# Grouping the expert work of a fused attention and mixture-of-experts kernel behind two of every three attention steps

## The chip, the cores and the metric

The kernel runs on one core of a Trainium2 chip. The metric is the device time of one execution in microseconds, as a median over runs. A profile is one further execution with the hardware profiler on; its own span is a little shorter than its device time, because the span runs from the first to the last instruction.

Five engines matter here. TensorE (PE in the views; PEld is its weight load) does matrix multiplies. VectorE (DVE) and ScalarE (ACT) do elementwise work, GpSimd (POOL) does one cast per step and issues the weight loads, and SyncE (SP) issues most other DMAs.

## The reference

Multi-query attention, 8 batches, 16 query heads that share one key and value head, 384 tokens, head size 64. The result is read as 3072 token rows of 1024 numbers and goes through a two-level mixture of experts: four groups, four experts in each, one expert per token.

```python
scores = scale * np.matmul(q, k.transpose(0, 1, 3, 2))
attn = softmax(scores)
x = np.matmul(attn, v)          # (B, H, S, D) -> rows (B*S, H*D)
...
g_idx = np.argmax(x @ w_group, axis=1)
e_idx = np.argmax(xg @ w_expert[g], axis=1)
h = np.maximum(xg[mask_e] @ w1[g, e], 0.0)
out[tok_idx] = (g_w * e_w)[:, None] * (h @ w2[g, e])
```

The kernel is built on the case that nearly all tokens of a batch choose the same expert: per batch it takes the most frequent expert of the first 128 tokens and runs all 384 tokens through it, gated. A single leftover pair of batch and expert is handled at the end in a compact form, and anything more in a rare block that these inputs do not enter.

## The kernel before

**Steps.** The attention is cut in 24 steps, `p = 0..23`, three for each batch `b` (`st = 0, 1, 2`: the opening, the middle and the last step of the batch). A step covers 128 query rows of all 16 heads. The whole order of work is written out by hand, and each engine executes its instructions in that order.

In step `p`, TensorE computes six score tiles (`scores`, L251, groups of four 64x64 matmuls in fp32) and, interleaved with them, the six value products of the step before (`values`, L290, accumulated in one PSUM tile `o`). The order is S0 S1 S2, V0 S3, V1 S4, V2, a small `join` (L273), S5, V3, V4, V5, where S belongs to step `p` and V to step `p-1`. ScalarE takes an exponential over each score tile (L253), then squares the raw queries for a later range check (`stats_q`, L209), and in the last step of a batch the keys also (`stats_k`, L213).

VectorE adds up the six exponentials (`pre_add`, L259 and L261), inverts the sums of the step before (L278, L280), multiplies the values product by them (`weigh`, L300, which frees `o`), folds its own sum (L265), and **turns**, that is transposes, the queries of the next step (`prep_q`, L243) and the keys of the next batch (`prep_k`, L233). In the text before the change these turns stand right behind S0 S1 S2 of each step.

**Phases.** Behind each step from the fifth on stands a phase of expert work. It is made of units, taken one by one from a queue by `fill(1)` (L451). A batch has 14 units: eight `h` units (L407, one 128-column block of the first layer, eviction on ScalarE in L408) and six `y` units (L415, eviction on ScalarE in L416, scaled by the gates `gsel`). Phases have four or five units; `FIVES` (L497) lists the steps with five. Three units are taken inside step 4.

**Gates.** In the phase of a middle step stand two further things. `gates(b)` (L466) multiplies the attention output by the gating weights (L312), and VectorE works out the choice of the expert and the gates (L318 to L382), with one exponential `ex` on ScalarE in between (L371). `counts(b, None)` (L333) counts the choices with one matmul (L338), copies the count on ScalarE (L342) and picks the expert on VectorE (L352); GpSimd then issues the loads of its weights. In the last step's phase `counts(None, b-1)` (L340, L342) and `gate_c` (L386 to L395) give `gsel` for the batch before.

**Buffers.** All PSUM tiles apart from `o` come from one pool of three (`side`, L76). A new tile waits for the last reader of the tile whose place it takes: an exponential, an eviction, a count copy, or VectorE's inversion.

**Loads.** In a middle step SyncE issues the keys of the next batch (L107), eight pieces of its queries (L92) and its values (L113), behind the stores of finished rows (L436).

Of the kernel before, what the change touches and what calls it, by code (L numbers as in the profile page):

```python
# [21 lines left out]
def kernel(  # L22
# [12 lines left out]
    B, H, S, D = q.shape  # L35
# [6 lines left out]
    ST = S // P  # L42
# [33 lines left out]
    def side(shape, dtype, name):  # L76
        return ps_s.tile(shape, dtype, tag="s", name=name)
# [20 lines left out]
    def some_q(n=1):  # L98
        for _ in range(n):
            if q_todo:  # L100
                q_todo.pop(0)()
# [129 lines left out]
    def prep_k(b):  # L231
        kT[b] = pool.tile([P, S], FP32, tag="kT", name="kT")
        nc.vector.transpose(out=kT[b][:], in_=k_raw[b][:].rearrange("p k d -> p (k d)"))  # L233

    def q_of(p):
        b, st = divmod(p, ST)
        if b == 0:
            return q_raw[0][:, st].rearrange("p h a d -> p h (a d)")
        return q_raw[b][:, :, st * (P // 32):(st + 1) * (P // 32)].rearrange("p h k d -> p h (k d)")

    def prep_q(p):
        qT[p] = pool.tile([P, 2 * CW], FP32, tag="qT", bufs=2, name="qT")
        nc.vector.transpose(out=qT[p][:].rearrange("p (h n) -> p h n", h=HP), in_=q_of(p))  # L243
# [71 lines left out]
    def gate_logits(b, ps, lo, hi):  # L315
        if lo == 0:
            logits[b] = pool.tile([P, ST, 32], FP32, tag="L", bufs=2, name="L")
        nc.vector.transpose(out=logits[b][:, lo:hi, :].rearrange("p s e -> p (s e)"), in_=ps[:, lo * 32:hi * 32])  # L318
# [14 lines left out]
    def counts(now, full):  # L333
        n = GE * (1 + ST)
        ps = side([P, n], FP32, "cps")
        lo, hi = (0 if now is not None else GE), (n if full is not None else GE)
        if now is not None:
            nc.tensor.matmul(out=ps[:, 0:GE], lhsT=ones_bf[:], rhs=first[now][:].rearrange("p g e -> p (g e)"), start=True, stop=True)  # L338
        if full is not None:
            nc.tensor.matmul(out=ps[:, GE:n], lhsT=ones_bf[:], rhs=ohe_t[full][:].rearrange("p s g e -> p (s g e)"), start=True, stop=True)  # L340
        t = pool.tile([P, n], FP32, tag="cnt1", bufs=2, name="cnt1")
        nc.scalar.copy(out=t[:, lo:hi], in_=ps[:, lo:hi])  # L342
        if now is not None:
            seen[now] = t[:, 0:GE]
            choose_b(now, t[:, 0:GE])
        if full is not None:
            gate_c(full, t[:, GE:n])

    def choose_b(b, cnt):
        top = pool.tile([P, 8], FP32, tag="top", bufs=1, name="top")  # L350
        idx = pool.tile([P, 8], U32, tag="idx", bufs=2, name="idx")
        nc.vector.max_with_indices(out_max=top[:], out_indices=idx[:], in_=cnt)  # L352
        reg = nc.values_load(idx[0:1, 0:1], engines=(ET.Pool,), min_val=0, max_val=GE - 1, skip_runtime_bounds_check_because="an index into 16 counts")
        w1 = wpool.tile([P, KO, F], BF16, tag="w1", name="w1")
        load_w1(w1, reg)
        w2 = wpool.tile([P, FO, Dm], BF16, tag="w2", name="w2")
        nc.gpsimd.dma_start(out=w2[:], in_=w2f[bass.ds(reg, 1)].rearrange("a p k f -> (a p) k f"))
        wts[b] = (w1, w2)
        choice[b] = idx
# [79 lines left out]
    NP = B * ST  # L439
# [26 lines left out]
    def gates(b):  # L466
        if b == 0:
            choose_a(0, gate_a(0, 0, 1))
            return
        ps = gate_a(b, 0, ST)  # L470
        choose_a(b, ps)
        gate_logits(b - 1, ps, 1, ST)
        gate_math(b - 1)
# [20 lines left out]
        nc.vector.tensor_copy(out=oki[:], in_=okf[:])  # L494
        bound["okf"] = okf

    FIVES = (8, 10, 12, 14, 16, 18, 19, 21, 22)  # L497
    leftover = {}

    def early_pair():  # L500
        last = B - 1
        mask = pool.tile([P, GE], FP32, tag="mask", bufs=1, name="mask1")
        idf = pool.tile([P, 1], FP32, tag="idf", bufs=1, name="idf1")
        nc.vector.tensor_copy(out=idf[:], in_=choice[last][:, 0:1])
        nc.vector.tensor_scalar(out=mask[:], in0=iota16[:], scalar1=idf[:, 0:1], scalar2=None, op0=OP.is_equal)
        nc.vector.scalar_tensor_tensor(out=extra[:, last * GE:NPAIR], in0=seen[last], scalar=0.0, in1=mask[:], op0=OP.is_gt, op1=OP.subtract)
        known = pool.tile([P, 1], FP32, tag="known", bufs=1, name="known")
        nc.vector.reduce_sum(out=known[:], in_=extra[:], axis=AX)
        top = pool.tile([P, 8], FP32, tag="top", bufs=1, name="top2")
        idx = pool.tile([P, 8], U32, tag="idx2", bufs=1, name="idx2")  # L510
        nc.vector.max_with_indices(out_max=top[:], out_indices=idx[:], in_=extra[:])
        pf = pool.tile([P, 1], FP32, tag="pf", bufs=1, name="pf")
        nc.vector.tensor_copy(out=pf[:], in_=idx[:, 0:1])
        base = pool.tile([P, 1], U32, tag="base", bufs=1, name="base")
        nc.vector.tensor_scalar(out=base[:], in0=idx[:, 0:1], scalar1=NPAIR - GE, scalar2=None, op0=OP.bitwise_and)
        basef = pool.tile([P, 1], FP32, tag="basef", bufs=1, name="basef")
        nc.vector.tensor_scalar(out=basef[:], in0=base[:], scalar1=float(S // GE), scalar2=None, op0=OP.mult)
        gi = pool.tile([P, ST, 2], FP32, tag="gi", bufs=1, name="gi")
        nc.vector.tensor_scalar(out=gi[:, :, 1], in0=tokid[:], scalar1=basef[:, 0:1], scalar2=None, op0=OP.add)
        reg = nc.values_load(idx[0:1, 0:1], engines=(ET.Pool, ET.DVE, ET.SP), min_val=0, max_val=NPAIR - 1, skip_runtime_bounds_check_because="an index into 128 flags")  # L520
        leftover.update(known=known, pf=pf, gi=gi, reg=reg)
# [16 lines left out]
    for p in range(NP):  # L538
        b, st = divmod(p, ST)
        jobs = [lambda: gates(0), lambda: None, lambda: counts(0, None)] if p == 2 else []  # L540
        if p == 0 or p == ST or (st == 1 and 1 < b < B - 1):
            load_q(b + 1)
        for j in range(3):
            scores(p, j)
            if p == 0 and j == 0:
                turn_q(1, lambda h: q_raw[0][:, 1, h], [nc.vector.tensor_copy])
        if p == 0:
            stats_k(0)
            prep_k(1)
        elif 2 < p < NP - 1:  # L550
            prep_q(p + 1)
            if st == 2:
                prep_k(b + 1)
        if jobs:
            jobs.pop(0)()
        for j in (1, 2):
            pre_add(p, j)
        for j in range(KB):
            if p > 0:
                values(p - 1, j)  # L560
            if j == 2 and p > 0:
                join(p - 1)
            if j + 3 < KB:
                scores(p, j + 3)
            if 0 < j < 4:
                pre_add(p, j + 2)
            if j == 2 and p > 0:
                invert(p - 1)
            if j == 3:
                stats_q(p)  # L570
                if p == 1:
                    turn_q(2, lambda h: q_raw[0][:, 2, h], [nc.scalar.copy])
                elif p == 2:
                    turn_q(3, lambda h: q_nat[0][:, h], [nc.scalar.copy])
            if jobs:
                jobs.pop(0)()
            if p == ST + 1 and j == 0:
                fill(3)
            if st == 1 and 0 < b < B - 1 and j == 0:
                load_k(b + 1)  # L580
            if 0 < j < 5:
                some_q(1 if p <= ST + 1 else 2)
            if st == 1 and b + 1 < B and j == KB - 1:
                load_v(b + 1)
        assert not jobs
        if p > 0:
            weigh(p - 1)
        fold_keys(p)
        if st == 2 and b + 1 < B:
            stats_k(b + 1)  # L590
        if p > ST:
            n = 5 if p in FIVES else 4
            steps = {}
            if p == NP - 1:
                bound_a()
            if st == 2:
                steps = {0 if b == 1 else 1: lambda: counts(None, b - 1)}
                if p == NP - 1:
                    steps = {0: lambda: (counts(None, b - 1), early_pair()), n - 1: bound_b}
            if st == 1:  # L600
                steps = {n - 2: lambda: gates(b), n - 1: lambda: counts(b, None)}
            for i in range(n):
                fill(1)
                if i in steps:
                    steps[i]()
# [250 lines left out]
```

## Time and profile before

| what | us |
|---|---|
| device time, three runs | 465.73, 466.64, 466.73 |
| device time of the profiled execution | 466.36 |
| its span | 464.9 |
| TensorE matmuls busy | 452.9 |
| VectorE busy | 305.4 |
| ScalarE busy | 243.0 |
| GpSimd busy | 60.4 |

The mean granted clock of TensorE was 0.995 of full speed. In the list of groups the first column is a line of the kernel, then come engine, operation, tiles and shapes, and after the bar the total busy time and the mean of one instruction in ns. A matmul's own duration says little, because consecutive ones overlap; what a stretch costs is read from the start of its first instruction to the start of the next stretch's first.

### The profile page before, as it was taken

How to read it: one execution, taken by the hardware profiler on the slowest of the kernel's cores; microseconds unless marked ns; L12 is line 12 of the kernel's file. 1: busy time of each engine (PE TensorE's matmuls, PEld its weight loads, DVE VectorE, ACT ScalarE, POOL GpSimd, SP SyncE). 2: the span in 40 equal slices, each digit the busy share in tenths (PEclk: the TensorE clock that was granted, in tenths of full speed). 3: DMA queues.
4: the chain of work that ended last, by engine and by line, in shares of the span. 5: the costliest groups of instructions: out<-in, count | busy, mean ns of one | idle time of the engine just before them, and what ended most of it. 6: DMA issues, size and time to landing. Idle time of an engine off the chain costs nothing. (4 is left out here: it accounts for less than half of the span.)

```text
span 464.9 us, 10115 instructions
## 1 busy us (share of the span) xinstructions
PE 452.9 (97%) x4175; PEld 197.6 (43%) x4191; DVE 305.4 (66%) x483; ACT 243.0 (52%) x351; POOL 60.4 (13%) x83
## 2 busy tenths in 40 slices
PE   8999999999999999999999999999999999999992
PEld 6343444433443344433534435434444334344641
DVE  3999958595795586783794865973867836774400
ACT  2966645556455555555475464564555554613331
POOL 1004003000130003000030001300030000330000
PEclk9999999999999999999999999999999999999997
DMA  8787997979399493967779494994929731499991
GB/s 156 104 135 112 217 214 127 205 171 233 66 164 233 166 158 51 202 129 244 132 113 211 124 191 101 159 203 172 165 61 205 139 158 47 77 210 262 284 248 70
DMA packets 152166, 74.57 MB, mean 160 GB/s; under 512 B 120216, under 2 KB 138652, under 8 KB 152112
## 3 DMA queue, kind: packets, MB, share of 16 engines
q0 software_dynamic: 28416, 37.84, 47.2%
q1 hardware_dynamic: 122368, 35.68, 32.4%
q8 instruction: 35, 0.57, 0.5%
q10 hardware_dynamic: 1328, 0.33, 0.4%
q14 instruction: 19, 0.16, 0.1%
HBM read 92.62 MB, written 19.01 MB: 240 GB/s over the span
## 5 line engine op out<-in xcount | busy, mean ns | idle before, releaser
L253 ACT ACTIVATE pt<-s 128x1024 f32<-128x1024 f32 x144 | 142.8, 1025 | 62.4 <-PE s L251 60.4
L251 PE MATMUL s<-qT,kT 64*64 64x512 f32 x1152 | 144.6, 597 | 0.3 <-ACT qT L229 0.2
L290 PE MATMUL o<-pt,v 64*64 64x512 f32 x1152 | 141.0, 590 | 0.0
L261 DVE TENSOR_TENSOR presum<-presum,pt 128x1024 f32<-128x1024 f32 x96 | 116.6, 1215 | 13.8 <-ACT pt L253 7.6
L407 PE MATMUL hps<-xbf,w 128*128 128x384 bf16 x512 | 88.3, 326 | 0.6 <-ACT hT L408 0.6
L415 PE MATMUL yps<-w,hT 128*128 128x512 bf16 x368 | 84.8, 379 | 0.8
L290 PEld LDWEIGHTS o<-pt,v 64*64 64x64 f32 x1152 | 43.5, 133 | 76.9 <-issue 76.5
L259 DVE TENSOR_TENSOR presum<-pt 128x1024 f32<-128x1024 f32 x24 | 29.1, 1211 | 67.0 <-ACT pt L253 66.9
L416 ACT ACTIVATE y<-yps,gsel 128x512 f32<-128x512 f32 x48 | 33.0, 687 | 67.5 <-PE yps L415 63.4
L251 PEld LDWEIGHTS s<-qT,kT 64*64 64x64 f32 x1152 | 39.0, 133 | 65.5 <-issue 52.6
L407 PEld LDWEIGHTS <-w 128*128 128x128 bf16 x512 | 47.9, 98 | 41.5 <-issue 10.4
L301 POOL CAST xbf<-xT 128x1024 bf16<-128x1024 f32 x24 | 25.0, 1041 | 294.9 <-DVE xT L300 294.9
L408 ACT ACTIVATE hT<-hps 128x384 bf16<-128x384 f32 x64 | 31.2, 488 | 56.2 <-PE hps L407 49.0
L415 PEld LDWEIGHTS <-hT 128*128 128x128 bf16 x384 | 36.5, 98 | 50.2 <-issue 8.1
L145 POOL DMA_DIRECT2D w<-in_moe_w_dram x36 | 24.8, 708 | 66.6 <-issue 49.2
L300 DVE TENSOR_TENSOR xT<-o,rinv 128x1024 f32<-128x1024 f32 x24 | 29.2, 1215 | 2.6 <-PE o L290 2.6
L280 DVE STREAM_TRANSPOSE rinv<-rc 128x1024 f32<-128x1024 f32 x24 | 29.9, 1246 | 0.8
L265 DVE TRANSPOSE_TENSOR_REDUCE fold<-presum 128x32 f32<-128x1024 f32 x24 | 29.6, 1232 | 0.0
L243 DVE STREAM_TRANSPOSE qT<-qraw 128x1024 f32<-128x1024 f32 x20 | 24.5, 1225 | 0.7
L209 ACT ACTIVATE qraw<-qraw 128x1024 f32<-128x1024 f32 x21 | 22.0, 1050 | 0.0
L318 DVE STREAM_TRANSPOSE L<-gps 128x32 f32<-128x32 f32 (+1 forms) x16 | 3.6, 227 | 27.9 <-PE gps L312 27.9
L273 PEld LDWEIGHTS sm<-fold,sel 64*64 64x64 f32 x192 | 7.2, 133 | 12.9 <-issue 12.9
(143 smaller groups left out, 157.7 us busy)
## 6 DMA issues: line engine op xcount, KB each, us to landing
w<-in_moe_w_dram POOLq DMA_DIRECT2D x36, 512.0 KB, 10.0
w<-in_moe_w_dram POOLq DMA_DIRECT2D x9, 2048.0 KB, 22.0
out_dram<-y SPq DMA_DIRECT2D x24, 512.0 KB, 3.2
qraw<-in_q_dram SPq DMA_DIRECT2D x56, 192.0 KB, 3.8
x_bf<-xbf SPq DMA_DIRECT2D x8, 768.0 KB, 3.3
v<-in_v_dram SPq DMA_DIRECT2D x16, 96.0 KB, 3.0
k<-in_k_dram SPq DMA_DIRECT2D x28, 48.0 KB, 2.6
qn<-in_q_dram SPq DMA_DIRECT2D x4, 256.0 KB, 4.8
```

The source lines that it names most:

```text
L251: nc.tensor.matmul(out=ps[64 * c:64 * c + 64, a, :], lhsT=kT[b][r, j * D:(j + 1) * D], rhs=qT[p][r, c * CW:(c + 1) * CW], start=True, stop ...
L253: nc.scalar.activation(out=t[:], in_=ps[:], func=ACTF.Exp, scale=scale)
L259: nc.vector.tensor_add(out=presum[p][:], in0=pt[p, 0][:], in1=pt[p, 1][:])
L261: nc.vector.tensor_add(out=presum[p][:], in0=presum[p][:], in1=pt[p, j][:])
L265: nc.vector.tensor_reduce(out=fold[p][:], in_=presum[p][:].rearrange("p a (n i) -> p (a n) i", i=32), axis=AX, op=OP.add, apply_transpose= ...
L280: nc.vector.transpose(out=t[:].rearrange("p (b i) -> p b i", i=32), in_=rc[:].rearrange("p c b -> p (c b)").unsqueeze(2).to_broadcast([P, ...
L290: nc.tensor.matmul(out=o_ps[p][64 * a:64 * a + 64, c, :], lhsT=v_sb[b][r, j, :], rhs=pt[p, j][r, a, :], start=(j == 0), stop=(j == KB - 1))
L300: nc.vector.tensor_mul(out=xT[b][:, :, ts], in0=o_ps[p][:].rearrange("p c (h n) -> p (c h) n", n=P), in1=rinv[p][:].rearrange("p (h n) -> ...
L407: nc.tensor.matmul(out=ps[:, 0:S], lhsT=w1[:, ko, fc * P:(fc + 1) * P], rhs=xb[:, ko, :], start=(ko == 0), stop=(ko == KO - 1))
L408: nc.scalar.activation(out=state["h"][:, fc, :], in_=ps[:, 0:S], func=ACTF.Relu)
L415: nc.tensor.matmul(out=ps[:], lhsT=state["h"][:, fo, st * P:(st + 1) * P], rhs=w2[:, fo, nh * CW:(nh + 1) * CW], start=(fo == 0), stop=(fo ...
L416: nc.scalar.activation(out=y, in_=ps[:], func=ACTF.Copy, scale=gs_of()[:, st:st + 1])
```

## The change

Phases stand only behind the opening and the middle step of a batch, from step 4 on, and behind the very last step. There are 14 of them in place of 20, with five to seven units each; the total of units in phases stays 89. The query and key turns leave the steps (apart from step 3) and are put in the phases on VectorE: in the phase of an opening or a middle step the query turn for the next step comes first, and in a middle step's phase the next batch's keys and first queries are turned behind the gates. The gates come behind the third unit of a middle phase, the count stays at its end. `counts(None, ...)` with `gate_c` moves from the last step's phase to the head of the next opening phase, ahead of the units.

```diff
-    FIVES = (8, 10, 12, 14, 16, 18, 19, 21, 22)
+    PHASES = {4: 5, 6: 7, 7: 6, 9: 7, 10: 6, 12: 7, 13: 6, 15: 7, 16: 6, 18: 7, 19: 6, 21: 7, 22: 7, 23: 5}
+
+    def gates_and_turns(p):
+        b = p // ST
+        gates(b)
+        if b + 1 < B:
+            prep_k(b + 1)
+            prep_q(p + 2)
...
-        elif 2 < p < NP - 1:
+        elif p == ST:
             prep_q(p + 1)
-            if st == 2:
-                prep_k(b + 1)
...
-        if p > ST:
-            n = 5 if p in FIVES else 4
+        if p in PHASES:
+            n = PHASES[p]
             steps = {}
-            if p == NP - 1:
+            if st < 2:
+                prep_q(p + 1)
+            if st == 0:
+                counts(None, b - 2)
+            elif st == 1:
+                steps = {2: lambda: gates_and_turns(p), n - 1: lambda: counts(b, None)}
+            else:
                 bound_a()
-            if st == 2:
-                steps = {0 if b == 1 else 1: lambda: counts(None, b - 1)}
-                if p == NP - 1:
-                    steps = {0: lambda: (counts(None, b - 1), early_pair()), n - 1: bound_b}
-            if st == 1:
-                steps = {n - 2: lambda: gates(b), n - 1: lambda: counts(b, None)}
+                steps = {0: lambda: (counts(None, b - 1), early_pair()), n - 1: bound_b}
             for i in range(n):
                 fill(1)
                 if i in steps:
```

## The prediction

> **What bounds the kernel now.** I read the busy line first, then the list of waits, then TensorE's timeline, and the other engines around its few losses. Timeline columns are start, duration, engine, line, operation, tiles, count; a bracket is the idle time before and its releaser.
>
> ```profile
> PE 452.9 (97%) x4175; PEld 197.6 (43%) x4191; DVE 305.4 (66%) x483; ACT 243.0 (52%) x351; POOL 60.4 (13%) x83
> ```
>
> Busy matmuls overlap, so 97% alone proves little. The timeline does: from 7.9 us to the tail each stretch of TensorE starts where the last one stops, so a microsecond saved there moves the end. What remains to be saved is at the seams. First a seam without a phase (step 3 to 4), then a phase (step 20):
>
> ```profile
> 47.75 2.75 PE L290 MATMUL o<-pt,v 64*64 64x512 f32 x24
> 50.32 2.75 PE L251 MATMUL s<-qT,kT 64*64 64x512 f32 x24
> 52.90 1.04 PE L290 MATMUL o<-pt,v 64*64 64x512 f32 x8
> ```
>
> ```profile
> 350.01 2.75 PE L290 MATMUL o<-pt,v 64*64 64x512 f32 x24
> 352.69 2.77 PE L407 MATMUL hps<-xbf,w 128*128 128x384 bf16 x16
> 355.30 0.19 PE L340 MATMUL cps<-ohe,ones_bf 128*128 128x48 bf16 x1
> 355.33 2.76 PE L407 MATMUL hps<-xbf,w 128*128 128x384 bf16 x16
> 358.02 2.81 PE L251 MATMUL s<-qT,kT 64*64 64x512 f32 x24
> 360.65 1.04 PE L290 MATMUL o<-pt,v 64*64 64x512 f32 x8
> ```
>
> Without a phase V3 to V5 take 50.32 - 47.75 = 2.57 us and S0 to S2 2.58. With one, the same and four h units take 360.65 - 350.01 = 10.64. An h unit is 1.30 (phases starting 170.40 and 225.03: four units 5.30, three 4.00), so the work is 2.57 + 5.20 + 2.58 = 10.35, and 0.29 is seam, 0.03 of it the count.
>
> The third view is the end of a middle phase (step 13):
>
> ```profile
> 231.80 0.17 PE L338 MATMUL cps<-ohe,ones_bf 128*128 128x16 bf16 x1
> ...
> 231.91 3.03 PE L251 MATMUL s<-qT,kT 64*64 64x512 f32 x24
> ...
> 232.31 0.25 ACT L371 ACTIVATE ex<-dl 128x60 f32<-128x60 f32 x1 [2.67 <-DVE dl L369]
> 232.47 0.47 ACT L408 ACTIVATE hT<-hps 128x384 bf16<-128x384 f32 x1
> ...
> 232.99 0.21 PEld L251 LDWEIGHTS s<-qT,kT 64*64 64x64 f32 x8 [0.87 <-ACT cnt L342]
> ```
>
> The gates' exponential sits on ScalarE 2.67 us for VectorE; the last h eviction is behind it, and S1, which takes that unit's PSUM place, behind both. V0 comes at 234.76, so S0 to S2 take 2.85, against 2.63 after other phases (358.02 to 360.65).
>
> **What the Trainium skill says.** "TensorEngine Tiling (Array Packing)", Key Properties: changing the tiling mode drains TensorE. The trace agrees: a seam between 64x64 and 128x128 work costs 0.26 us there and back, one inside 64x64 work nothing. "TensorE: Matmul & The Clock Gate", Architectural detail: ScalarE and VectorE are strict first in, first out. The exit above shows it. "Perfetto Trace Analysis", Identifying the Most-Contended Engine: matmul occupancy is a poor measure of distance to roofline; hence the reading by start times.
>
> **The change part by part.** Units, matmuls, exponentials, adds, turns and DMAs stay the same in number. P is a phase's start, T a step's.
>
> *1. Six phases less* (steps 5, 8, 11, 14, 17, 20). The same sum over them, with a y unit at 1.73 (five take 8.74, four 7.01), gives seams of 0.28, 0.28, 0.29, 1.00, 0.29, 0.29. Less 0.03 for the count, which is moved, and with the 1.00 taken as 0.29: 6 x 0.26 = **1.56 us gained**, all on TensorE's path.
>
> *2. The 1.00.* In step 14:
>
> ```profile
> 245.52 0.49 ACT L408 ACTIVATE hT<-hps 128x384 bf16<-128x384 f32 x1 [0.81 <-PE cps L340]
> ...
> 246.06 2.76 PE L407 MATMUL hps<-xbf,w 128*128 128x384 bf16 x16 [0.56 <-ACT hT L408]
> ```
>
> The unit behind the count takes the PSUM place of the unit just before and waits for its eviction, 0.71 us over a normal seam. In the changed program's order no unit takes its direct predecessor's place: **0.71 gained**.
>
> *3. Gates earlier.* They come behind unit 3 of 5 to 7, with two to four units between them and the count. `ex` ends about 7.5 us after P (232.56 - 225.03); the phases last 8.2 or more. The eviction is no longer late at the exit: 7 x (2.85 - 2.63) = **1.6 gained**. Inside the phase one h eviction waits until about P+8.0; its place is wanted again at P+8.3 in the shortest phase, P+9.4 in the others, so nothing is lost.
>
> *4. Counts at the head of opening phases.* One matmul, one copy and six small VectorE operations, as before, but VectorE now does weigh, fold and the query turn first. In step 12's phase (P = 205.71) the turn ended at 209.84, P+4.13; `gate_c` takes 1.1 (192.80 to 193.91). `gsel` is ready at about P+5.25, the first y eviction at P+6.0. Queued behind it are later evictions; who waits is the fourth unit, if the first is a y. That is so in step 6 alone (units 9 to 14 are y): the fourth would start at 0.15 + 3 x 1.73 = P+5.35 and can start at P+6.1, **0.75 lost**. In step 9 an h unit comes first and the fourth y starts at P+6.65; later phases have more h units. For the count's price at a phase's head I take its 0.03; at most its 0.11 of an exit (231.80 to 231.91), 0.5 in all; below nothing is excluded.
>
> *5. Turns.* VectorE did turns at T+2.1 to T+3.9 in last steps, ahead of the adds:
>
> ```profile
> 234.04 1.25 DVE L243 STREAM_TRANSPOSE qT<-qraw 128x1024 f32<-128x1024 f32 x1
> 235.21 0.54 DVE L233 STREAM_TRANSPOSE kT<-k 128x384 f32<-128x384 f32 x1
> 235.67 1.18 DVE L259 TENSOR_TENSOR presum<-pt 128x1024 f32<-128x1024 f32 x1
> ...
> 244.55 1.23 DVE L265 TRANSPOSE_TENSOR_REDUCE fold<-presum 128x32 f32<-128x1024 f32 x1
> ```
>
> Now they follow the gates: these end at 233.56, P+8.5; keys to P+9.0, queries to P+10.25, expert choice to P+10.7. The adds of the next step can start at T+3.2 (306.58 for T = 303.39), that is P+11.4 or later. So the turns cost nothing; the phase's matmuls hide them. They wait for eight query pieces that SyncE issues in the same step: in step 13 the last was issued at 226.36 and the median landing is 3.8, so 230.2, and the turn is reached at 234.1, as before. The weights are asked for 1.8 us later in a phase and used two steps later at the earliest.
>
> *6. Steps without a phase.* VectorE's step back to back is 10.1 us (235.67 to 245.78), TensorE's 10.4 (39.90 to 50.32). In step 17 weigh ended at T+12.4 (315.82 - 303.39); without a phase the next V0 comes at T + 10.4 + 2.6 = T+13.0. So it fits with 0.6 to spare, and step 3 to 4 shows it fitting with a query turn in the step. ScalarE needs 6 x 1.02 + 1.24 + 0.7 = 8.1. Cost taken: nothing; upper bound 0.4 per seam, 2.4.
>
> Sum: -1.56 - 0.71 - 1.6 + 0.75 = **-3.1 us**. Against its own span: 464.9 to 461.8. The profiled execution (466.36) lies inside the three runs, so the median goes from 466.64 to **463.5**.
>
> **The rivals.**
>
> *A, one gain missing:* ScalarE or the `o` tile makes V0 wait at seams without a phase and eats the 1.56, or `ex` still delays the exits (1.6). For it: VectorE has 0.3 us of room per step. Against: step 3 to 4. 463.5 + 1.6 = 465.1.
>
> *B, no change:* both missing; the waits move from seam to seam. 463.5 + 3.1 = 466.6.
>
> *C, slower:* VectorE becomes the bound at the six seams. The next batch's query turn now stands ahead of the expert choice and all adds in an in-order queue and waits for DMAs. If they land late, weigh is late, V0 waits for `o`, and TensorE stands still six times. It decides from a weigh later than T+13.0; to end 0.2% slower the six must lose 3.1 + 0.9 = 4.0 us, 0.67 each, a weigh some 1.3 us later than in step 17: one more large VectorE instruction. At 1 us each: 463.5 + 6 = 469.5. For it: one query piece once took 24.5 us to land. Against: the 4 us between landing and turn.
>
> **How the numbers follow.** 0.2% (0.9 us) is about what a measurement of this kernel can tell from no change. Main case 0.70, with 0.6 either way for item 4 and a placement of PSUM tiles I misread; A 0.14; B 0.08; C 0.08. The range from 462.6 to 465.8 holds main and A. Faster by over 0.2% (below 465.7): 0.83; within: 0.09; slower: 0.08.
>
> **What would show it.** Right: V3-V5 followed directly by S0-S2 in steps 5, 8, 11, 14, 17, 20, with V0 2.6 us after S0; exits of middle phases at 2.63; no wait of a score's weight load on the count copy; one pause of about 0.75 in step 6's phase. Wrong: V0 waiting for VectorE's xT (C), for pt (A), or pauses in opening phases other than step 6's.

## The result, and the profile after

The changed kernel takes 463.09 us (median of six runs, 462.54 to 463.63), the kernel before 466.62 beside it (six runs, 465.73 to 466.98). The ratio is 0.9928, with a 95% interval from 0.9915 to 0.9941. The profiled execution took 463.58 with a span of 462.0 at a mean clock of 0.994; the span before was 464.9. On the page of the changed kernel the busy line is

```profile
PE 450.8 (98%) x4191; PEld 199.3 (43%) x4191; DVE 305.7 (66%) x483; ACT 242.6 (53%) x351; POOL 60.4 (13%) x83
```

VectorE and ScalarE are as busy as before; only TensorE's time got shorter. To see where, a measure is needed that leaves the opening out: the first `h` units of step 4 start anywhere between 54.43 and 55.22 us in the profiled executions of this study, though TensorE has the same instructions ahead of them. (The last experiment moves these units and gets ends of its own.) I call **stretch** the time from there to the last 48 value products behind step 23. What follows scatters too: from these products to the end of the span it is 51.01 to 52.18 us. These are its two ends in TensorE's timeline, of the kernel before and of the changed one:

```profile
54.73 4.07 PE L407 MATMUL hps<-xbf,w 128*128 128x384 bf16 x24
...
413.01 5.36 PE L290 MATMUL o<-pt,v 64*64 64x512 f32 x48
```

```profile
54.93 4.08 PE L407 MATMUL hps<-xbf,w 128*128 128x384 bf16 x24
...
410.07 5.36 PE L290 MATMUL o<-pt,v 64*64 64x512 f32 x48
```

The stretch was 413.01 - 54.73 = 358.28 us and is 410.07 - 54.93 = 355.14, so 3.14 us less. The prediction's sum was 3.1. The device times differ by 3.53 us, and their interval (0.59% to 0.85%, 2.8 to 4.0 us) holds the 3.14. The views that the prediction named follow, all of the changed kernel. A seam without a phase (step 5 to 6, TensorE's timeline):

```profile
81.29 2.75 PE L290 MATMUL o<-pt,v 64*64 64x512 f32 x24
83.87 2.75 PE L251 MATMUL s<-qT,kT 64*64 64x512 f32 x24
86.44 1.04 PE L290 MATMUL o<-pt,v 64*64 64x512 f32 x8
```

V3 to V5 take 2.58 and S0 to S2 take 2.57: nothing is lost here, and the other five such seams have the same two numbers. The end of a middle phase (step 13), first on TensorE, then on ScalarE:

```profile
228.66 4.07 PE L407 MATMUL hps<-xbf,w 128*128 128x384 bf16 x24
232.57 0.17 PE L338 MATMUL cps<-ohe,ones_bf 128*128 128x16 bf16 x1
232.67 2.81 PE L251 MATMUL s<-qT,kT 64*64 64x512 f32 x24
235.30 1.04 PE L290 MATMUL o<-pt,v 64*64 64x512 f32 x8
```

```profile
230.47 0.25 ACT L371 ACTIVATE ex<-dl 128x60 f32<-128x60 f32 x1 [2.68 <-DVE dl L369]
230.63 0.47 ACT L408 ACTIVATE hT<-hps 128x384 bf16<-128x384 f32 x1
231.47 0.49 ACT L408 ACTIVATE hT<-hps 128x384 bf16<-128x384 f32 x1 [0.37 <-PE hps L407]
232.77 0.49 ACT L408 ACTIVATE hT<-hps 128x384 bf16<-128x384 f32 x1 [0.81 <-PE cps L338]
```

The exponential still waits 2.68 us for VectorE, and one `h` eviction still sits behind it. But now two more units follow, and their evictions start as soon as their matmuls are done. V0 comes 235.30 - 232.67 = 2.63 us after S0, where it was 2.85. All seven exits read 2.62 or 2.63. In the list of waits (total us, times, longest) two lines answer to this and to the counts:

```profile
ACT y L416 <- DVE gsel L395: 9.9, 3, 4.8
...
PEld s L251 <- ACT cnt L342: 0.9, 2, 0.4
```

The score's weight loads waited 6.1 us in seven places for the count copy before; two waits of 0.4 remain, with five of at most 0.4 for an `h` eviction, and they delay no V0. The `y` evictions now wait longer for `gsel` (before: 2.0 us, one time). What that costs is seen in step 6's phase, on TensorE and on VectorE:

```profile
94.40 0.20 PE L340 MATMUL cps<-ohe,ones_bf 128*128 128x48 bf16 x1
94.44 5.34 PE L415 MATMUL yps<-w,hT 128*128 128x512 bf16 x24
100.36 5.34 PE L415 MATMUL yps<-w,hT 128*128 128x512 bf16 x24 [0.58 <-ACT y L416]
```

```profile
96.17 1.23 DVE L265 TRANSPOSE_TENSOR_REDUCE fold<-presum 128x32 f32<-128x1024 f32 x1
97.33 1.20 DVE L243 STREAM_TRANSPOSE qT<-qraw 128x1024 f32<-128x1024 f32 x1
98.45 0.16 DVE L386 TENSOR_REDUCE cnt<-cnt 128x16 f32<-128x48 f32 x1
...
99.32 0.20 DVE L395 TENSOR_REDUCE gsel<-gm 128x3 f32<-128x48 f32 x1
```

The first three `y` units take 100.36 - 94.44 = 5.92 us in place of 3 x 1.73 = 5.19: 0.73 is lost, because `gsel` ends at P+5.1, behind fold and turn. No other opening phase has a pause.

### The profile page after: what moved, and what is told of

Read it like the earlier page. It is cut to its first block, busy times and chain, and to the rows that moved or that the text cites. A ratio compares the mean times of both kernels' runs of the same rounds, so it can differ in the third digit from the quotient of the medians.

```text
span 462.0 us, 10131 instructions
## 1 busy us (share of the span) xinstructions
PE 450.8 (98%) x4191; PEld 199.3 (43%) x4191; DVE 305.7 (66%) x483; ACT 242.6 (53%) x351; POOL 60.4 (13%) x83
## 5 line engine op out<-in xcount | busy, mean ns | idle before, releaser
L251 PE MATMUL s<-qT,kT 64*64 64x512 f32 x1152 | 142.8, 595 | 0.2 <-ACT qT L229 0.2
L251 PEld LDWEIGHTS s<-qT,kT 64*64 64x64 f32 x1152 | 40.2, 133 | 64.3 <-issue 52.2
L243 DVE STREAM_TRANSPOSE qT<-qraw 128x1024 f32<-128x1024 f32 x20 | 24.1, 1202 | 0.0
```

The lines of the kernel that those rows point to most:

```text
L251: nc.tensor.matmul(out=ps[64 * c:64 * c + 64, a, :], lhsT=kT[b][r, j * D:(j + 1) * D], rhs=qT[p][r, c * CW:(c + 1) * CW], start=True, stop ...
```

## The experiments

The device times are medians, the ratio is to the kernel before on the same chip. The stretch is read from the trace as above.

| kernel | us | ratio (95%) | stretch, us |
|---|---|---|---|
| before | 466.62 | | 358.28 |
| changed | 463.09 | 0.9928 (0.9915 to 0.9941) | 355.14 |
| changed, gates late | 464.87 | 0.9967 (0.9956 to 0.9979) | 356.73 |
| before, gates early | 464.61 | 0.9961 (0.9947 to 0.9975) | 356.71 |
| changed, counts first | 462.21 | 0.9918 (0.9905 to 0.9931) | 354.39 |
| changed, turns in the steps | 462.79 | 0.9925 (0.9912 to 0.9938) | 354.75 |
| changed, one more turn | 464.45 | 0.9952 (0.9940 to 0.9965) | 356.32 |
| changed, two more turns | 472.00 | 1.0121 (1.0106 to 1.0135) | 364.03 |
| changed, a 128x128 matmul at six seams | 464.82 | 0.9967 (0.9954 to 0.9980) | 356.79 |
| changed, a 64x64 matmul at six seams | 463.64 | 0.9934 (0.9921 to 0.9946) | 355.73 |
| before, count behind the first unit | 468.08 | 1.0040 (1.0026 to 1.0054) | 359.73 |
| before, count later in step 14 | 465.70 | 0.9990 (0.9984 to 0.9997) | 357.58 |
| changed, counts first, and step 4's units together | 462.38 | 0.9918 (0.9905 to 0.9931) | see below |

### Is it the place of the gates that shortens the exits?

One part undone in the changed kernel. The gates, with the turns behind them, again come ahead of the last unit of a middle phase, so that a single unit follows them:

```diff
-                steps = {2: lambda: gates_and_turns(p), n - 1: lambda: counts(b, None)}
+                steps = {n - 2: lambda: gates_and_turns(p), n - 1: lambda: counts(b, None)}
```

> The changed kernel with the gates (and the turns behind them) put back to where the gates stood before: two units ahead of a middle phase's end. Theory: the exponential of the gates again holds up the last h eviction at the exit, and with it S1; the seven exits of middle phases go from 2.63 back to about 2.85 us, in all +1.6 us over the changed kernel, about 464.7. Rival: the exits were shortened by something else that came with the change (fewer phases, another order of PSUM places); then they stay at 2.63 and the time at 463.1.

And the gates alone moved forward in the kernel before, by one unit in phases of four and by two in phases of five:

```diff
-                steps = {n - 2: lambda: gates(b), n - 1: lambda: counts(b, None)}
+                steps = {1: lambda: gates(b), n - 1: lambda: counts(b, None)}
```

> The kernel before with one edit: the gates of a middle phase come behind the second unit in place of the third or second from the end. Theory: this alone shortens the seven exits of middle phases from 2.85 to 2.63 us, -1.6 us, about 465.0, with the phases of all three steps kept. Rival: the exits are long because a phase of four or five units is too short for the gates' chain wherever it stands; then 466.6.

Undone, the kernel takes 464.87 us, and all seven exits are back at 2.85 or 2.86. In step 13, on TensorE and on ScalarE:

```profile
233.31 3.04 PE L251 MATMUL s<-qT,kT 64*64 64x512 f32 x24
236.17 1.04 PE L290 MATMUL o<-pt,v 64*64 64x512 f32 x8
```

```profile
233.71 0.25 ACT L371 ACTIVATE ex<-dl 128x60 f32<-128x60 f32 x1 [2.68 <-DVE dl L369]
233.87 0.47 ACT L408 ACTIVATE hT<-hps 128x384 bf16<-128x384 f32 x1
```

Now the exponential starts 0.40 us after S0, and the eviction that S1 needs comes behind it. The stretch grew by 356.73 - 355.14 = 1.59 us, which is seven times 0.23. Done alone, the same kind of shift gave 358.28 - 356.71 = 1.57 us and exits of 2.62 or 2.63, with all 20 phases in place and phases of only four or five units. In step 13, where the gates moved by one unit, TensorE shows

```profile
231.72 2.81 PE L251 MATMUL s<-qT,kT 64*64 64x512 f32 x24
234.34 1.04 PE L290 MATMUL o<-pt,v 64*64 64x512 f32 x8
```

So the length of a phase isn't what matters, and about half of the whole gain belongs to this one line.

### What does a phase cost at its seams?

A tiny matmul is put at the six seams without a phase. It is one instruction with 16 columns, its result unread, once in the units' tiling and once in the attention's:

```diff
+        if st == 0 and p > ST:
+            dm = side([P, CW], FP32, "dm")
+            nc.tensor.matmul(out=dm[:, 0:16], lhsT=ones_bf[:], rhs=ones_bf[:, 0:16], start=True, stop=True)
```

> The changed kernel with one tiny 128x128 bf16 matmul (16 columns, result unread) between V5 and S0 at the six seams without a phase. Theory (what a phase costs at its seams is the change between 64x64 and 128x128 work): +0.15 to +0.26 us at each, about +1.3 us, 464.4. Rival (it is waits of the phase's units, not the crossing): about 0.03 us at each, +0.2, 463.3.

```diff
+        if st == 0 and p > ST:
+            dm = side([P, CW], FP32, "dm")
+            nc.tensor.matmul(out=dm[0:64, 0:16], lhsT=sel2[0:64].rearrange("p a b -> p (a b)"), rhs=sel2[0:64, 0, 0:16], start=True, stop=True)
```

> The control for that: at the same six places an equally small 64x64 fp32 matmul (16 columns, result unread), so the same PSUM place is taken and no change of tiling is made. Theory: 0.03 to 0.05 us at each, +0.2 to 0.3 in all, 463.3. If it costs as much as the 128x128 one, the cost was not the crossing but the additional instruction and its PSUM place.

The 128x128 matmul in TensorE's timeline, step 11 to 12:

```profile
188.54 2.75 PE L290 MATMUL o<-pt,v 64*64 64x512 f32 x24
191.23 0.18 PE L553 MATMUL dm<-ones_bf 128*128 128x16 bf16 x1
191.34 2.81 PE L251 MATMUL s<-qT,kT 64*64 64x512 f32 x24
193.97 1.04 PE L290 MATMUL o<-pt,v 64*64 64x512 f32 x8
```

From V3 to V0 it is 193.97 - 188.54 = 5.43 us, against 5.15 without it: 0.28 at each seam, and 356.79 - 355.14 = 1.65 in the stretch (1.3 expected). The seam has the signature of a real phase: V3 to V5 take 0.11 more before the foreign matmul starts, and S0 to S2 take 2.63 in place of 2.57. No engine is waited for. The same seam with the 64x64 matmul in it, which starts at 190.60:

```profile
188.02 2.75 PE L290 MATMUL o<-pt,v 64*64 64x512 f32 x24
...
193.23 1.08 PE L290 MATMUL o<-pt,v 64*64 64x512 f32 x8
```

From V3 to V0 it is 5.21 us, 0.06 more than without it; a further 0.03 to 0.04 comes at the end of the step, where V3 to V5 take 2.72 in place of 2.69. The stretch is longer by 355.73 - 355.14 = 0.59, or 0.10 each, more than the 0.03 to 0.05 expected; the matmul runs as two instructions with two weight loads (12 more loads on the page). It takes the same PSUM place as the 128x128 one, so the place isn't the cost. The crossing from 64x64 to 128x128 work and back is thus worth between 0.28 - 0.10 = 0.18 us and 0.25 (0.28 less the 0.03 that such a matmul takes inside 128x128 work). The prediction's 0.26 per phase is just above that.

The two tiny matmuls differ in their data type too, as the units and the attention do: the 128x128 work is bf16, the 64x64 work fp32. The opening of the kernel before separates the two in part, because there the queries are transposed by 128x128 matmuls in fp32 between value products in fp32 (step 2, V2 ahead, V4 and V5 behind):

```profile
36.14 1.04 PE L290 MATMUL o<-pt,v 64*64 64x512 f32 x8
37.11 1.09 PE L228 MATMUL qps<-ident,qe 128*128 128x128 f32 x8
38.14 1.95 PE L290 MATMUL o<-pt,v 64*64 64x512 f32 x16
39.90 2.75 PE L251 MATMUL s<-qT,kT 64*64 64x512 f32 x24
```

One value product takes 0.86 us among others of its tiling (42.48 to 43.34 in the same trace). Here the one ahead takes 0.97 and the two behind 1.76, so 0.11 and 0.04 more, nearly what the bf16 crossing shows on its two sides, with the data type unchanged. What a change of type alone costs, no run shows.

### Where is the loss in step 6's phase from?

```diff
+            if st == 0:
+                counts(None, b - 2)
             if st < 2:
                 prep_q(p + 1)
-            if st == 0:
-                counts(None, b - 2)
-            elif st == 1:
+            if st == 1:
...
```

> The changed kernel with the count and gate_c of an opening phase ahead of the query turn on VectorE; nothing else. Theory: gsel is ready about 1.2 us earlier (P+3.9 in place of P+5.1), ahead of the first y eviction's possible start, so the pause of 0.58 us (0.73 lost) in step 6's phase goes: -0.7 us against the changed kernel, about 462.4. Rival: the pause has another cause (the PSUM places of consecutive y units alone); then it stays, and the time with it.

It was 462.21 us, as expected. In step 6's phase of this kernel TensorE shows the six `y` units as one stretch:

```profile
93.94 10.52 PE L415 MATMUL yps<-w,hT 128*128 128x512 bf16 x48
104.29 1.46 PE L407 MATMUL hps<-xbf,w 128*128 128x384 bf16 x8
```

That is 104.29 - 93.94 = 10.35 us, 6 x 1.73 = 10.38. The stretch is 0.75 us shorter than the changed kernel's. So the pause came from a late `gsel`, and the turn ahead of it was enough to make it late.

### Do the turns have to leave the steps?

```diff
-        elif p == ST:
+        elif 2 < p < NP - 1:
             prep_q(p + 1)
+            if st == 2:
+                prep_k(b + 1)
```

(and the turns in the phases taken out)

> The changed kernel with the query and key turns left in the steps behind S0 to S2, as in the kernel before; phases, gates and counts as changed. Theory: the turns cost nothing in either place, since VectorE runs ahead of TensorE by more than a turn at each seam without a phase; and in step 6 gate_c no longer stands behind a query turn, so its pause goes: 462.3 to 463.1. Rival (VectorE is the bound at the seams without a phase unless the turns leave the steps): weigh comes later there by up to 1.2 us, V0 waits for it, six times: 466 to 470.

It was 462.79 us, and no seam lost anything: the six still read 2.57 and 2.58. VectorE in step 11, where the step begins at T = 179.31 and the next at 189.77:

```profile
180.58 1.25 DVE L243 STREAM_TRANSPOSE qT<-qraw 128x1024 f32<-128x1024 f32 x1
181.75 0.54 DVE L233 STREAM_TRANSPOSE kT<-k 128x384 f32<-128x384 f32 x1
182.43 1.23 DVE L259 TENSOR_TENSOR presum<-pt 128x1024 f32<-128x1024 f32 x1 [0.15 <-ACT pt L253]
...
190.53 1.22 DVE L300 TENSOR_TENSOR xT<-o,rinv 128x1024 f32<-128x1024 f32 x1
```

The first add starts at T+3.12 and weigh ends at 191.75, T+12.44. In the changed kernel these are T+3.13 and T+12.43: there VectorE stands idle for 1.99 us ahead of that add, waiting for the exponentials, and the turns fit in that hole. So the move of the turns, the most visible part of the change, gains nothing. The stretch is even 0.39 us shorter, since in step 6's phase `gsel` no longer stands behind a query turn and the pause falls from 0.58 to 0.20 us. It doesn't go altogether: the turn now stands in the step, ahead of its adds, and weigh, fold and then `gsel` come later for it. `gsel` ends at P+4.75, against P+5.12 in the changed kernel and P+3.99 with the counts first.

### How much room has VectorE at a seam without a phase?

One redundant query turn, or two, behind the first two adds of the last steps of batches 1 to 6:

```diff
+        if st == 2 and ST < p < NP - 1:
+            for _ in range(1):
+                nc.vector.transpose(out=qT[p + 1][:].rearrange("p (h n) -> p h n", h=HP), in_=q_of(p + 1))
```

> The changed kernel with one redundant query turn (about 1.2 us of VectorE, writing the same values once more) behind the first two additions of the last step of batches 1 to 6: the six steps without a phase behind them. Theory: VectorE's room at such a seam is 0.6 us before weigh makes V0 wait, and about as much again is given back by the wait of the adds for the exponentials, so 1.2 us more costs about 0.3 us at each, +1.8 us in all, 464.9 (range 463.1 to 467). Rival (VectorE has a whole phase of slack, nothing decides at the seam): no change, 463.1. Rival (VectorE is the bound already): 6 x 1.2 = +7.2, 470.

> The same with two redundant turns, 2.4 us of VectorE at each of the six seams. Theory: past the room, all of the second turn shows: about 1.5 us at each, +9 us, 472. If there is no room at all: +14. If VectorE's room is more than 2.4 us at such a seam: no change, 463.1.

They took 464.45 and 472.00 us. At step 11 to 12, VectorE's weigh and TensorE's S0 and V0 with one turn, and then the same with two:

```profile
192.50 1.21 DVE L300 TENSOR_TENSOR xT<-o,rinv 128x1024 f32<-128x1024 f32 x1
```

```profile
191.13 2.75 PE L251 MATMUL s<-qT,kT 64*64 64x512 f32 x24
193.77 1.09 PE L290 MATMUL o<-pt,v 64*64 64x512 f32 x8
```

```profile
195.96 1.21 DVE L300 TENSOR_TENSOR xT<-o,rinv 128x1024 f32<-128x1024 f32 x1
```

```profile
193.29 2.75 PE L251 MATMUL s<-qT,kT 64*64 64x512 f32 x24
197.22 1.09 PE L290 MATMUL o<-pt,v 64*64 64x512 f32 x8 [1.18 <-DVE xT L300]
```

Step 11 begins at T = 180.66 with one turn and at 182.82 with two. Weigh then ends at T+13.05 and T+14.35, against T+12.43 in the changed kernel: 0.62 and 1.92 later. V0 follows 0.05 or 0.06 us behind it in both, and comes 2.64 and 3.93 us after S0, so 0.07 and 1.36 are lost. The loss there is the delay less 0.55: that is the room, and past it every microsecond by which weigh is late is one of TensorE. In both, V0 itself also takes 0.05 longer up to S3 (0.91 in place of 0.86). Of the first turn's 1.2 us, half went into waits for exponentials that the adds had anyway. In the stretch the first turn costs 1.18 and the second 7.71 more. Of the first turn's 1.18, the longer pause in step 6's phase (0.92) has 0.33; the six seams have the rest, 0.14 each, half of what was expected of them.

### The wait in step 14

In the kernel before:

```diff
-                steps = {0 if b == 1 else 1: lambda: counts(None, b - 1)}
+                steps = {0: lambda: counts(None, b - 1)}
```

> The kernel before with one edit: the count of a last step's phase comes behind the first unit in all batches, not behind the second. Theory: in step 14 the unit behind the count no longer takes the PSUM place of the unit just before it, and the wait of 0.56 us (0.71 over a normal seam) goes: -0.7 us, about 465.9. Rival: the wait moves to another unit or another phase as the order of PSUM places shifts: 466.6.

This missed: 468.08 us, slower than before. The wait stayed in step 14, and the same wait came up in steps 8 and 11. TensorE in step 8's phase:

```profile
134.49 1.47 PE L407 MATMUL hps<-xbf,w 128*128 128x384 bf16 x8
135.80 0.19 PE L340 MATMUL cps<-ohe,ones_bf 128*128 128x48 bf16 x1
136.54 2.76 PE L407 MATMUL hps<-xbf,w 128*128 128x384 bf16 x16 [0.56 <-ACT hT L408]
```

I had the order of PSUM places wrong: with the count behind the first unit, the unit behind the count waits for the eviction of the unit just before it in three phases, not in none. The price of it holds. From V3 to S0 step 8's phase takes 10.88 in place of 10.17 and step 11's 9.15 in place of 8.44, 0.71 each, and the stretch grew by 359.73 - 358.28 = 1.45. The second attempt moved the count the other way, in step 14 alone:

```diff
-                steps = {0 if b == 1 else 1: lambda: counts(None, b - 1)}
+                steps = {0 if b == 1 else 2 if b == 4 else 1: lambda: counts(None, b - 1)}
```

> The kernel before with one edit, in step 14 alone: the count comes behind the third unit of the phase, not behind the second. In the program as it is built, the unit behind the count then takes the place of an inversion that was long done, and the count that of the unit two before it. Theory: the wait of 0.56 us goes and nothing else comes, step 14's phase is 0.71 us shorter, -0.7 us: about 465.7. Rival: the count's own place, freed by an eviction only 1.3 us earlier, gives a wait of the same kind, or the later gsel holds up the y unit and S1 at the exit: 466.4.

TensorE in step 14's phase of that kernel:

```profile
242.72 4.08 PE L407 MATMUL hps<-xbf,w 128*128 128x384 bf16 x24
246.63 0.19 PE L340 MATMUL cps<-ohe,ones_bf 128*128 128x48 bf16 x1
246.65 1.46 PE L407 MATMUL hps<-xbf,w 128*128 128x384 bf16 x8
247.95 1.89 PE L415 MATMUL yps<-w,hT 128*128 128x512 bf16 x8
```

The wait is gone, and S0 follows the phase at 249.77, so that V3 to S0 take 9.74 us in place of 10.46. The stretch is 0.70 shorter. The device time, 465.70 (21 runs) against 466.28 (25 runs), agrees: 0.58 us less, with an interval from 0.14 to 0.75 us by the ratio.

### A version past the changed kernel

Counts first, as above, and the three units inside step 4 moved into its phase:

```diff
-    PHASES = {4: 5, 6: 7, 7: 6, 9: 7, 10: 6, 12: 7, 13: 6, 15: 7, 16: 6, 18: 7, 19: 6, 21: 7, 22: 7, 23: 5}
+    PHASES = {4: 8, 6: 7, 7: 6, 9: 7, 10: 6, 12: 7, 13: 6, 15: 7, 16: 6, 18: 7, 19: 6, 21: 7, 22: 7, 23: 5}
...
-            if p == ST + 1 and j == 0:
-                fill(3)
```

> The count and gate_c ahead of the query turn, as in the experiment on that alone, and the three units that are taken inside step 4 moved into step 4's phase (eight units there). Theory: -0.73 for step 6's pause and one crossing between 64x64 and 128x128 work less, -0.26: about 462.1. Rival: the three units inside step 4 fill a wait of TensorE there (for the first exponentials), so taking them out costs that wait, and the time is 462.4 or more.

It was 462.38 us, which the scatter of the runs doesn't tell from the 462.21 of counts first alone. The traces do: from step 4's S0 to the last value products it is 408.69 - 50.16 = 358.53 us, against 408.82 - 50.03 = 358.79. One crossing less gave the expected 0.26, and the steps around it have no new wait. Both versions beat the kernel before. Against the changed one their ratios are lower by 0.001, 0.5 us, with intervals that overlap, so the device times alone don't show a gain; the stretches say 0.75 for the count, and 0.26 more for the merged units.

## Why the prediction was right

The time forecast was 463.5 us, measured were 463.09; the sum of gains was 3.1, the stretch shows 3.14. Single executions of one kernel differ by about 1 us, so that the device time came this near is in part luck; the terms of the stretch carry the argument. Point by point:

1. **Six phases less** (1.56). The seams without a phase lose nothing, and one crossing costs 0.18 to 0.25 by the added matmuls and 0.26 by the one taken away. With the three other terms as measured, the stretch leaves 3.14 - 0.71 - 1.57 + 0.73 = 1.59 for the six. That it is the crossing, not an engine waited for, was read from two seams of the kernel before; the pair of tiny matmuls shows it. That the tiling and not the data type makes the crossing costly rests on the transposes in the opening alone.
2. **The wait in step 14** (0.71). Gone in the changed kernel, 0.70 when it is taken away alone, 0.71 for each one added. The mechanism was right. That no unit of the changed program would wait so came true as well, but it was the less secure half: the next guess of the same kind, with the count behind the first unit, failed.
3. **Gates earlier** (1.6). 1.59 undone, 1.57 done alone.
4. **Counts at the head of opening phases** (0.75 lost). 0.73, in step 6 alone as named, and 0.75 comes back when the count goes ahead of the turn. The count itself takes 0.04 there in place of the 0.03 assumed.
5. **Turns** (nothing, apart from the one ahead of `gsel` in item 4). Shown from both sides: left in the steps they cost nothing at the seams either. The prediction put it on the phase's matmuls that hide them; in the steps the wait for the exponentials hides them just as well.
6. **Steps without a phase** (nothing, 0.6 us of room). The room is 0.55.

Of the rivals, A and B needed one or both gains to be missing, and neither was. C was right about its mechanism and its threshold: weigh about 1.2 us later loses 0.67 at a seam, by the line found above. But it counted one more large VectorE instruction as such a delay, and one turn delayed weigh by only 0.62, since the adds had waits to give. It takes two to make the kernel slower than before. The late query piece that spoke for C had two late companions (10.8 to 24.5 us to landing, and 11.0 to 24.1 in the changed kernel), all issued between 38 and 55 us, ahead of the first of the six seams. The query pieces issued from 105 us on took 5.7 us at most in the changed kernel, and at every such seam V0 came on time.

## What to carry to other kernels

Where TensorE has no gap left, read the few seams at which its tiling or its partner changes, price each from the start of one stretch to the start of the next, and count how many the new order has; the sum of such small terms forecast this kernel to a few tenths of a microsecond. Within a group of work on one in-order engine, ask what stands ahead of the small result that another engine waits for: moving the gates forward by one or two units was worth as much as removing six phases, and moving the count ahead of one transpose half as much. The part of a change with the most lines (here the turns) may be worth nothing, if it only moves work from one hole into another.

## What I had not expected of the hardware

Nothing of the engines contradicted the earlier trace. Two things were new to me. The opening of the kernel, with the same instructions, took 54.43 to 55.22 us in different profiled executions, a scatter as large as the smaller two of the four terms here; only a stretch with fixed ends shows them. The traces say where it arises, though not why: the 18 warm-up matmuls of L442 start at 4.51 or 4.52 us in every execution, and the work behind them starts 1.14 to 1.92 us later; from the first score matmul to the first `h` unit it is again 46.87 to 46.95 us in all twelve kernels that keep those units there. And the place that a PSUM tile gets isn't a plain rotation of the three, as far as the waits show: in a rotation the third `h` unit of step 14 in the kernel before would have taken the place of the first, whose eviction was over at 244.71, but it started at 246.06, just behind the second's eviction (245.52 to 246.01). Moving one small tile by one unit brought the same wait up in two phases that had not had it.
